# A second-layer quarter moved behind four columns of the next batch's first layer, and a second layer that starts in another PSUM bank

## The chip, the cores and the metric

The kernel runs on one core of a Trainium2 chip. The metric is the device time of one execution in microseconds (us), taken over five runs. Engines are named as in the profile: PE multiplies matrices, PEld loads its weights, DVE is the vector engine, ACT the scalar engine, POOL (GpSimd) issues the loads, SP issues the transposing DMAs and the stores.

## The reference

Eight batches of 448 tokens, 12 heads of 64, so d_model is 768; d_ff is 3072. Squared-ReLU attention, then a layer norm, a two-layer network and a residual:

```python
scores = scale * np.matmul(q, k.transpose(0, 1, 3, 2))
attn = np.maximum(scores, 0.0) ** 2 / S
x = np.matmul(attn, v)                       # then heads side by side: (B, S, 768)
mu, var = np.mean(x, -1), np.mean((x - mu) ** 2, -1)
xn = (x - mu) / np.sqrt(var + 1e-06) * g_ln
out = x + np.maximum(xn @ w_ch1, 0.0) @ w_ch2
```

All products run in bf16 with fp32 sums.

## The kernel before

The program is written out by hand, engine by engine: each engine executes its instructions in the order in which the Python code emits them, and waits on semaphores for what it needs. So a line of Python that is emitted earlier stands earlier in the queue of its engine.

The network of batch b and the attention of batch b+1 run interleaved. `ffn_1_all(b)` (L842) loops over the 24 columns `ni` of the hidden layer, each 128 of the 3072 hidden units. A column is 12 matmuls (L447): six slices `ki` of d_model, times two halves of 64 output partitions that run side by side on the array. ACT then evicts the column with a ReLU into row `ni` of `h` (L449). Between the columns stand "excursions" (L836): three score products of the next batch (L296, L301), their ReLU by ACT (L311, L305) and DVE (L307) and their squares by DVE (L314), and the products with v (L331). In batch 1 they stand behind columns 3, 6, 9, 13, 15, 18 and 21 (`IN_SECOND`).

From batch 2 on the last four columns are computed by `unit` (L649) with seven products instead of eight, in four PSUM banks called c, d, a and e; its products are L660, its evictions L671 to L690. Bank e is read for the last time by DVE at L687, bank c at L676, bank a by the second L671.

The second layer of batches 1 to 7, `ffn_2_all` (L935), takes pairs of 128-token tiles and does each pair in seven products (L515) of 24 matmuls, in three banks that go around. Their order is this line (L941), where x and y are the two banks of the turn `f_turn` and z is `spare[0]`:

```python
banks = [x_bank, z_bank, y_bank]
```

After `unit`, x is its bank c, y its bank e and z its bank a. Batch 4 alone has one pair; there the kernel skips one bank of the turn (`next_f()`, L943), so that the next column starts in the other one.

The second layer of batch 0, `ffn_2_first` (L904), is done plainly, because the weights of the second layer `w2` are still arriving: blocks B11, B21, B12 and B22, 1152 KB each, are loaded by POOL in this order (L214). `plain_part` (L489) does one part of the 24 slices of the hidden layer for tile m and half dh of the output; parts are quarters. For dh=1 the order is m0 and m1 with the first two quarters (block B12), then m0 and m1 with the last two (block B22). Each tile's sum stays in one bank of the turn until DVE evicts it (`scaled_plus`, L482). Between the parts stand the centering of batch 1's input on DVE (L411), a copy of 192 columns of `h` (`carry`, L458) and sums of weight blocks on DVE (`w2_sums`, L218), which batch 1's seven products need.

What feeds the scores of the next batch is a chain of DMAs: POOL loads q and k of a head pair i into one of three slots of `qk_ring` (L175 to L177), SP transposes them into `qkT` (L260, three buffers), PE reads that. The loads of pair i+3 wait until pair i is transposed. On SP's queue also stand the transposes into `x_tok` (L424) and the stores (L475); those of batch 0 are held back until column 9 of batch 1 (`held_stores`, L880).

Of the kernel before, what the change touches and what calls it, by code (L numbers as in the profile page):

```python
# [11 lines left out]
def kernel(  # L12
# [11 lines left out]
    P = 128  # L24
# [3 lines left out]
    Alu = mybir.AluOpType  # L28

    B, H, S, D = q.shape  # L30
# [12 lines left out]
    K2 = d_ff // P  # L43
    KH = K2 // 2
# [37 lines left out]
    w2 = big_pool.tile([P, 7, KH, HD], bf16)  # L82
    B11, B22, B12, B21, B_SUM, B_TOP, B_BOT = range(7)
# [44 lines left out]
    next_f = f_turn.next  # L128
    spare = fb[2:]
# [86 lines left out]
    def w2_sums(slot, a, b, op, part):  # L216
        r = slice(part * KH // 2, (part + 1) * KH // 2)
        nc.vector.tensor_tensor(w2[:, slot, r], w2[:, a, r], w2[:, b, r], op=op)  # L218
# [195 lines left out]
    def tiles_of(b):  # L414
        return range(b * S // P, (b + 1) * S // P)

    def x_slot(m):
        b = next(b for b in range(B) if m in tiles_of(b))
        return m - tiles_of(b)[0] + (0 if b % 2 else 4)
# [6 lines left out]
    def x_carry(b):  # L426

        nc.scalar.copy(xT[:, :, :D], x_first[:, :, S - D:] if b == 0 else xT[:, :, S:])
# [13 lines left out]
    def ffn_1(ni, bank=None):  # L442
        ps = (next_f() if bank is None else bank)[:, :S]
        for ki in range(K1):
            for c in range(2):
                n0 = ni * P + c * D
                nc.tensor.matmul(ps[c * D:(c + 1) * D, :], w1[:, ki, n0:n0 + D], xc[:, ki, :],  # L447
                                 start=(ki == 0), stop=(ki == K1 - 1))
        nc.scalar.activation(h[:, ni, CARRY:], ps, Act.Relu)  # L449

    def h_cols(b, m):
        c0 = CARRY + m * P - b * S
        return slice(c0, c0 + P)
# [6 lines left out]
    def new_o():  # L460
        o_t = o_pool.tile([P, HD], fp32, tag="o")
        return o_t

    def new_acc():
        acc_t = acc_pool.tile([P, HD], fp32, tag="acc")
        return acc_t
# [14 lines left out]
    def scaled_plus(o_t, y, m, plus):  # L481
        nc.vector.scalar_tensor_tensor(o_t, y, rstd[:, m:m + 1], plus, op0=Alu.mult, op1=Alu.add)  # L482

    def x_half(m, dh):
        return x_tok[:, x_slot(m), dh * HD:(dh + 1) * HD]

    held_stores = []

    def plain_part(b, m, dh, part, parts, box):  # L489
        if part == 0:  # L490
            box[m] = next_f()[:, :HD]
        n = K2 // parts
        cols = h_cols(b, m)
        for ki in range(part * n, (part + 1) * n):
            slot = ((B11, B12), (B21, B22))[ki // KH][dh]
            for c in range(2):
                t0 = cols.start + c * D
                nc.tensor.matmul(box[m][c * D:(c + 1) * D, :], h[:, ki, t0:t0 + D],  # L498
                                 w2[:, slot, ki % KH, :], start=(ki == 0), stop=(ki == K2 - 1))
        if part == parts - 1:  # L500
            o_t = new_acc() if dh else new_o()
            scaled_plus(o_t, box[m], m, x_half(m, dh))
            held_stores.append(lambda: store(o_t, m, dh * HD, (dh + 1) * HD))

    s_turn = Turns(range(3))
# [222 lines left out]
    ready = []  # L728
# [113 lines left out]
    def ffn_1_all(b):  # L842
        ms = tiles_of(b)
        for ni in range(NI0 if b == 0 else 0, UNIT if b >= UNIT_FROM else K2):
            if b == 0 and ni == NI0:
                ffn_1_first()
            if b == 0 and ni == NI0 + 2:
                x_carry(0)
            if b == 0 and ni == X_AT[0]:

                nc.sync.dma_start(held, h[:1, ni - 1, CARRY:CARRY + 16])
            if b == 0 and ni in X_AT:
                ffn_x(b, X_AT.index(ni))
            if b == 0 and ni == IN_FIRST[-1] + 1:
                flush_loads()
            if b == 0 and ni in V_AT:
                load_v(V_AT[ni])
            bursts = (IN_FIRST, IN_SECOND, IN_REST)[min(b, 2)]
            ffn_1(ni, spare[1] if b < B - 1 and ni in bursts and len(ready) > 1 else None)
            flush()  # L860
            at = STATS_AT[min(b, 2)][:len(ms)]
            if ni in at:
                ffn_stats(ms[at.index(ni)])
            if b >= UNIT_FROM:
                for n in X_SUMS_AT.get(ni, ()):
                    x_sum(n)
            if b == 1 and ni in SUMS_AT:
                w2_sums(*LATE_SUMS[SUMS_AT.index(ni)])
            if b == 0:
                if ni in IN_FIRST:  # L870
                    excursion(3)
                if ni == IN_FIRST[-1] + 3:
                    next_AV(bank=spare[1])
                if ni in T_IN_FIRST:
                    att_T(NPAIR + T_IN_FIRST[ni])
            elif b < B - 1:
                if ni in bursts:
                    first = nc.vector if b > 1 and ni == bursts[0] else nc.scalar
                    excursion(3, third=(first, nc.vector), **(dict(evac_by=nc.scalar) if b == 1 else {}))
                    while ni > bursts[1] and held_stores:  # L880
                        held_stores.pop(0)()
                if b == 1 and ni == K2 - 1:
                    flush_loads()
                    next_AV(bank=spare[1])

        late = []

        def between(n):
            if n == 2:
                flush_loads()  # L890
            if n == 3:
                next_AV(bank=sc_turn.items[0][:, 0], evac_by=nc.scalar, later=late)
            if n == 5:
                posts.extend(late)

        if b >= UNIT_FROM:
            unit(between)

    CENTER_AT = (4, 6, 8)
    SUMS_AT = (0, 1, 2, 4, 7, 11)  # L900
    LATE_SUMS = [(o, x, y, op, part)
                 for o, x, y, op in ((B_BOT, B21, B22, Alu.add), (B12, B12, B22, Alu.subtract),
                                     (B21, B21, B11, Alu.subtract)) for part in range(2)]
    def ffn_2_first():  # L904
        b = 0
        ffn_rstd(b)
        box = {}
        assert not ready
        steps = center(1)
        n = 0  # L910
        for dh in range(2):

            order = [(m, part) for m in range(2) for part in range(4)]
            if dh:
                order.sort(key=lambda x: x[1] // 2)
            for m, part in order:
                plain_part(b, m, dh, part, 4, box)
                if n < K1 - 1:
                    gain(1, n)
                if n == 3:  # L920
                    gain(1, K1 - 1)
                if n in CENTER_AT:
                    steps[CENTER_AT.index(n)]()
                if n == 2:
                    for ki in range(K1):
                        ffn_x(1, ki)
                if n == 8:
                    carry(b)
                if n in (9, 10):
                    w2_sums(B_TOP, B11, B12, Alu.add, n - 9)  # L930
                if n in (13, 15):
                    w2_sums(B_SUM, B11, B22, Alu.add, (n - 13) // 2)
                n += 1

    def ffn_2_all(b):  # L935
        ffn_rstd(b)
        x_bank, y_bank = f_turn.items
        z_bank = spare[0]
        first = b * S // (2 * P)
        pairs = range(first, (b + 1) * S // (2 * P))  # L940
        banks = [x_bank, z_bank, y_bank]  # L941
        if len(pairs) == 1:
            next_f()  # L943
        todo = []
        if b < B - 1:
            assert not ready
            todo = [lambda k=k: (gain(b + 1, k), gain(b + 1, k + 1)) for k in range(0, K1, 2)]
            todo += center(b + 1)
            if b % 2:
                todo.append(lambda: x_carry(b + 1))  # L950

        def between(n):
            n += 7 * (pr - first)
            if n == (8 if len(pairs) == 2 else 1):
                carry(b)
                if b < B - 1:
                    for ki in range(K1):
                        ffn_x(b + 1, ki)
            if todo:
                todo.pop(0)()  # L960
            if b == UNIT_FROM - 1 and n >= 8 and n < 13:
                w1_sum(n - 8)

        for pr in pairs:
            last = b == B - 1 and pr == pairs[-1]
            seven(b, pr, banks, last, between)
            banks = banks[1:] + banks[:1]
        assert not todo
# [70 lines left out]
```

## Time and profile before

| | |
|---|---|
| median of 5 runs | 521.96 us (521.66 to 522.72) |
| the profiled execution's own time | 522.72 us |
| its span, first to last instruction | 520.6 us, so 2.1 us lie around it |
| PE busy | 510.5 us (98%), granted clock 1.00 throughout |
| DVE busy | 390.3 us (75%) |
| ACT busy | 288.5 us (55%) |
| POOL busy | 224.3 us (43%) |

The times of instructions below come from the one profiled execution and count from its first instruction. A matmul's row shows when it starts and when its result is through; the next one starts well before that, so a PE that reads busy all the time can still lose time between two starts. "Idle before" in a row of the timeline is counted from the end of the last instruction, and is shown from 0.15 us on.

### The profile page before, as it was taken

To read this page: it belongs to the slowest core of one execution; us is meant where nothing else is said; L and a number is where in the kernel's file an instruction comes from. 1 tells how busy PE (TensorE), PEld (TensorE's weight loads), DVE (VectorE), ACT (ScalarE), POOL (GpSimd) and SP (SyncE) were. 2 spreads that over 40 slices of the span, in tenths; PEclk is the share of its full clock that TensorE was granted. 3 is DMA by queue.
4 is the path that set the end of the run, shared out by engine and by line. 5 is a ranking of instruction groups with operands and counts; after the bars stand their busy time and mean duration, and the time that the engine had idled before them with its cause. 6 is when DMAs were issued, how large, how long until landed. Compare 5 with 4: busy or idle time off the path is not lost.

```text
span 520.6 us, 14156 instructions
## 1 busy us (share of the span) xinstructions
PE 510.5 (98%) x5902; PEld 344.2 (66%) x5902; DVE 390.3 (75%) x696; ACT 288.5 (55%) x489; POOL 224.3 (43%) x257
## 2 busy tenths in 40 slices
PE   8999999999999999999999999999999999999996
PEld 4355566546765588755887558655886558877885
DVE  6966779868988689687886868987796867970554
ACT  6986632786248762487524875577525774244220
POOL 9727114778533753248432485257532000320031
PEclk9999999999999999999999999999999999999999
DMA  9999999999537992579924799279924300240022
GB/s 134 181 199 200 184 204 157 147 198 111 82 88 108 121 83 66 117 72 134 82 69 102 77 129 137 64 88 112 85 69 101 62 1 3 79 106 1 3 62 62
DMA packets 175280, 53.05 MB, mean 102 GB/s; under 512 B 154224, under 2 KB 175216, under 8 KB 175216
## 3 DMA queue, kind: packets, MB, share of 16 engines
q0 software_dynamic: 103712, 25.75, 52.9%
q1 hardware_dynamic: 70976, 26.03, 27.0%
q8 instruction: 46, 0.75, 0.6%
q10 hardware_dynamic: 528, 0.37, 0.2%
q14 instruction: 18, 0.15, 0.1%
HBM read 51.91 MB, written 11.01 MB: 121 GB/s over the span
## 4 chain that ended last, share of the span: by engine, by line
PE 80%; DMA 13%; POOL 3%; ACT 2%; DVE 1%; issue 1%; POOLq 0%; ACTq 0%
PE f L515 34%; PE f L447 31%; DMA w<-in_moe_w_ch_dram 7%; PE f L331 4%; DMA s_sb<-in_v_dram 4%; PE f L660 3%; PE sc L301 3%; PE f L301 1%; DMA qkT_t<-qk_ring 1%; DMA v_ring<-in_v_dram 1%; PE sc L296 1%; PE f L498 1%; DVE s_sb L676 1%; PE sc L331 1%; PE f L354 1%; ACT h L675 1%
## 5 line engine op out<-in xcount | busy, mean ns | idle before, releaser
L447 PE MATMUL f<-xc,w 128*64 128x448 bf16 x1968 | 198.3, 353 | 0.3
L447 PEld LDWEIGHTS <-w 128*64 128x64 bf16 x1968 | 114.8, 110 | 76.6 <-issue 15.1
L449 ACT ACTIVATE h<-f 128x448 bf16<-128x448 f32 x164 | 90.3, 551 | 75.3 <-PE f L447 70.2
L515 PE MATMUL f<-w,s_sb 128*64 128x384 bf16 (+2 forms) x1584 | 130.4, 324 | 0.0
L515 PEld LDWEIGHTS <-s_sb 128*64 128x64 bf16 x1584 | 107.9, 110 | 19.3
L311 ACT ACTIVATE at<-sc 128x896 bf16<-128x896 f32 x120 | 103.0, 917 | 5.6 <-PE sc L301 5.1
L314 DVE TENSOR_TENSOR at<-at 128x896 bf16<-128x896 bf16 x168 | 96.8, 619 | 6.9 <-ACT at L311 6.2
L548 POOL TENSOR_TENSOR o_t<-o_t,x_tok 128x384 f32<-128x384 f32 x26 | 24.9, 956 | 153.9 <-ACT o_t L547 153.9
L175 POOL DMA_DIRECT2D qk_ring<-in_q_dram x36 | 46.7, 1298 | 82.0 <-DMA qkT_t<-qk_ring 56.6
L547 ACT ACTIVATE o_t<-f,rstd 128x384 f32<-128x384 f32 x26 | 15.1, 581 | 94.7 <-DVE acc_t L552 37.1
L509 DVE TENSOR_TENSOR s_sb<-h 128x1536 bf16<-128x1536 bf16 x65 | 64.3, 1005 | 0.0
L176 POOL DMA_DIRECT2D qk_ring<-in_k_dram x36 | 55.8, 1550 | 11.1 <-DMA w<-in_moe_w_ch_dram 11.1
L515 PE MATMUL f<-w,h 128*64 128x384 bf16 x624 | 53.2, 326 | 0.9 <-DVE s_sb L676 0.2
L177 POOL DMA_DIRECT2D qk_ring<-in_k_dram x36 | 46.9, 1303 | 4.8 <-DMA w<-in_moe_w_ch_dram 4.7
L515 PEld LDWEIGHTS <-h 128*64 128x64 bf16 x624 | 42.7, 110 | 9.3 <-issue 1.9
L307 DVE TENSOR_SCALAR at<-f 128x448 bf16<-128x448 f32 x59 | 35.6, 616 | 15.0 <-PE f L301 15.0
L548 POOL TENSOR_TENSOR acc_t<-acc_t,x_tok 128x384 f32<-128x384 f32 x24 | 29.0, 1216 | 21.3 <-ACT acc_t L547 21.3
L187 POOL DMA_DIRECT2D v_ring<-in_v_dram x36 | 32.5, 1170 | 0.5 <-DMA qk_ring<-in_q_dram 0.3
L331 PE MATMUL f<-at,v_ring 128*64 128x448 bf16 x248 | 31.1, 357 | 1.2 <-DMA v_ring<-in_v_dram 1.2
L411 DVE SCALAR_TENSOR_TENSOR xc<-f,g_sb,xc 128x448 bf16<-128x448 f32 x45 | 28.5, 678 | 4.6 <-PE f L405 4.6
L301 PE MATMUL sc<-qkT_t 64*128 64x448 bf16 x192 | 30.0, 356 | 0.0
L370 DVE TENSOR_SCALAR xT<-f 128x448 bf16<-128x448 f32 x22 | 13.6, 617 | 18.4 <-ACT at L311 9.8
(111 smaller groups left out, 525.9 us busy)
## 6 DMA issues: line engine op xcount, KB each, us to landing
w<-in_moe_w_ch_dram POOLq DMA_DIRECT2D x6, 768.0 KB, 13.0
w<-in_moe_w_ch_dram POOLq DMA_DIRECT2D x4, 1152.0 KB, 29.5
v_ring<-in_v_dram POOLq DMA_DIRECT2D x21, 192.0 KB, 5.2
qk_ring<-in_q_dram POOLq DMA_DIRECT2D x36, 112.0 KB, 5.1
qk_ring<-in_k_dram POOLq DMA_DIRECT2D x36, 96.0 KB, 4.9
out_dram<-o_t SPq DMA_DIRECT2D x8, 168.0 KB, 2.2
out_dram<-acc_t SPq DMA_DIRECT2D x7, 168.0 KB, 2.2
out_dram<-o_t SPq DMA_DIRECT2D x8, 144.0 KB, 2.1
```

The lines of the kernel that those rows point to most:

```text
L175: nc.gpsimd.dma_start(q_to, q[b, heads].rearrange("x (p j) d -> p j x d", j=NJ))
L176: nc.gpsimd.dma_start(k_to[:, :NF], k[b, heads, :SF].rearrange("x (p t) d -> p t x d", t=NF))
L177: nc.gpsimd.dma_start(k_to[:SS, NF], k[b, 2 * a:2 * a + 2, SF:].rearrange("x s d -> s x d"))
L301: nc.tensor.matmul(by_j(half[hh]), k_of(i, r, t, P), q_of(i, r), start=True, stop=True)
L311: nc.scalar.activation(at, ps[:, :, :S], Act.Relu)
L314: nc.vector.tensor_mul(attn[i, t], attn[i, t], attn[i, t])
L331: nc.tensor.matmul(ps[hh * D:(hh + 1) * D, :], weights, values, start=start, stop=stop)
L447: nc.tensor.matmul(ps[c * D:(c + 1) * D, :], w1[:, ki, n0:n0 + D], xc[:, ki, :], start=(ki == 0), stop=(ki == K1 - 1))
L449: nc.scalar.activation(h[:, ni, CARRY:], ps, Act.Relu)
L509: nc.vector.tensor_tensor(s_sb[:, n], x, y, op=op)
L515: nc.tensor.matmul(ps[c * D:(c + 1) * D, :d1 - d0], stat[:, ki, c * D:(c + 1) * D], w2[:, slot, ki, d0:d1], start=(start and ki == 0), sto ...
L548: nc.gpsimd.tensor_tensor(o_t, o_t, x_half(m, dh), op=Alu.add)
```

## The change

In batch 0's second layer, half dh=1 stops after the two quarters that use block B12; DVE evicts each of the two partial sums with the residual into an fp32 tile (`first_halves`). The two quarters that use B22 become a sum of their own, in banks taken anew from the turn, and run behind column 3 of batch 1's first layer (`ffn_2_first_rest`), ahead of the excursion there; a second `scaled_plus` adds them to the tile. The weight sum B_SUM moves from between those quarters into batch 1's columns 1 and 2, and B_BOT moves from columns 0 and 1 to column 3, where the first half of the new B12 (before at column 2) stands too.

In all later second layers the three banks start with y in place of x. The skipped turn after batch 4 is gone; instead the first column of batch 5 takes `spare[1]`.

```diff
     held_stores = []
+    first_halves = {}
 
     def plain_part(b, m, dh, part, parts, box):
-        if part == 0:
+
+        parted = dh and part == parts // 2
+        if part == 0 or parted:
             box[m] = next_f()[:, :HD]
...
                 nc.tensor.matmul(box[m][c * D:(c + 1) * D, :], h[:, ki, t0:t0 + D],
-                                 w2[:, slot, ki % KH, :], start=(ki == 0), stop=(ki == K2 - 1))
+                                 w2[:, slot, ki % KH, :], start=ki == 0 or bool(dh and ki == KH),
+                                 stop=ki == K2 - 1 or bool(dh and ki == KH - 1))
+        if dh and part == parts // 2 - 1:
+            first_halves[m] = new_acc()
+            scaled_plus(first_halves[m], box[m], m, x_half(m, dh))
         if part == parts - 1:
-            o_t = new_acc() if dh else new_o()
-            scaled_plus(o_t, box[m], m, x_half(m, dh))
+            o_t = first_halves[m] if dh else new_o()
+            scaled_plus(o_t, box[m], m, first_halves[m] if dh else x_half(m, dh))
             held_stores.append(lambda: store(o_t, m, dh * HD, (dh + 1) * HD))
...
-            ffn_1(ni, spare[1] if b < B - 1 and ni in bursts and len(ready) > 1 else None)
+
+            late = ni == 0 and b > 1 and b * S // (2 * P) - (b - 1) * S // (2 * P) == 1
+            ffn_1(ni, spare[1] if late or b < B - 1 and ni in bursts and len(ready) > 1 else None)
...
-            if b == 1 and ni in SUMS_AT:
-                w2_sums(*LATE_SUMS[SUMS_AT.index(ni)])
+            if b == 1:
+                for n, part in enumerate(p for p, at in zip(LATE_SUMS, SUMS_AT) if at == ni):
+                    if ni == REST_AT and n < 2:
+                        ffn_2_first_rest(n)
+                    w2_sums(*part)
...
-    SUMS_AT = (0, 1, 2, 4, 7, 11)
+
+    REST_AT = 3
+    SUMS_AT = (1, 2, 3, 3, 3, 4, 7, 11)
     LATE_SUMS = [(o, x, y, op, part)
-                 for o, x, y, op in ((B_BOT, B21, B22, Alu.add), (B12, B12, B22, Alu.subtract),
-                                     (B21, B21, B11, Alu.subtract)) for part in range(2)]
+                 for o, x, y, op in ((B_SUM, B11, B22, Alu.add), (B_BOT, B21, B22, Alu.add),
+                                     (B12, B12, B22, Alu.subtract), (B21, B21, B11, Alu.subtract))
+                 for part in range(2)]
...
         for dh in range(2):
-
-            order = [(m, part) for m in range(2) for part in range(4)]
-            if dh:
-                order.sort(key=lambda x: x[1] // 2)
-            for m, part in order:
+            for m, part in [(m, part) for m in range(2) for part in range(2 if dh else 4)]:
                 plain_part(b, m, dh, part, 4, box)
...
                 if n in (9, 10):
                     w2_sums(B_TOP, B11, B12, Alu.add, n - 9)
-                if n in (13, 15):
-                    w2_sums(B_SUM, B11, B22, Alu.add, (n - 13) // 2)
                 n += 1
 
+    def ffn_2_first_rest(m):
+        for part in (2, 3):
+            plain_part(0, m, 1, part, 4, box_rest)
+
+    box_rest = {}
...
-        banks = [x_bank, z_bank, y_bank]
-        if len(pairs) == 1:
-            next_f()
+        banks = [y_bank, z_bank, x_bank]
```

## The prediction

> **What bounds the kernel now.** First the page's busy line: which engine fills the span.
>
> ```profile
> PE 510.5 (98%) x5902; PEld 344.2 (66%) x5902; DVE 390.3 (75%) x696; ACT 288.5 (55%) x489; POOL 224.3 (43%) x257
> ```
>
> PE does. The change gives PE the same matmuls, so only PE's waits can change. Next, PE's waits from 40 us on (total, times, longest):
>
> ```profile
> PE f L498 <- DMA w<-in_moe_w_ch_dram: 0.8, 1, 0.8
> PE sc L296 <- DMA qkT_t<-qk_ring: 0.5, 1, 0.5
> PE f L515 <- DVE s_sb L676: 0.2, 1, 0.2
> ```
>
> Three places: block B22 landing late, pair 17's transposed q and k landing late, and a PSUM bank that DVE frees late. This view counts idle time from the end of the last matmul; I count from start to start, with PE's timeline (start, length, instruction). Around B22 and around pair 17:
>
> ```profile
> 72.75 6.99 PE L498 MATMUL f<-w,h 128*64 128x384 bf16 x84
> 80.50 4.09 PE L498 MATMUL f<-w,h 128*64 128x384 bf16 x48 [0.76 <-DMA w<-in_moe_w_ch_dram]
> 84.40 4.73 PE L447 MATMUL f<-xc,w 128*64 128x448 bf16 x48
> 89.06 0.55 PE L301 MATMUL sc<-qkT_t 64*128 64x448 bf16 x4
> ...
> 113.03 0.35 PE L296 MATMUL sc<-qkT_t 64*64 64x448 bf16 x2
> 113.84 0.38 PE L296 MATMUL sc<-qkT_t 64*64 64x448 bf16 x2 [0.46 <-DMA qkT_t<-qk_ring]
> ```
>
> The 48 matmuls of L498 start at 80.50 and the next kind at 84.40, so a pair (two halves side by side) takes 3.90 / 24 = 0.163 us, while one lasts 0.326. The last pair before the wait ended at 79.74, so it started at 79.41 and the next could have started at 79.575: B22 costs 80.50 - 79.575 = 0.93 us. The four L296 at 104.32 all start within 0.01 us, so the wait at 113.04 costs 0.80 us. The chain of waits names its cause, a transpose that SP issued at 107.64 and that landed at 113.80.
>
> The third place is at the end of FFN1's seven products, here in batch 2 (PE, then DVE):
>
> ```profile
> 187.08 0.74 PE L660 MATMUL f<-s_sb,w 128*64 128x224 bf16 x12
> 187.97 2.30 PE L515 MATMUL f<-w,h 128*64 128x384 bf16 x26
> ...
> 185.97 0.62 DVE L687 TENSOR_TENSOR s_sb<-f,s_sb 128x448 f32<-128x448 f32 x1
> 187.29 0.62 DVE L676 TENSOR_TENSOR s_sb<-s_sb,f 128x448 f32<-128x448 f32 x1 [0.70 <-ACT h L675]
> 188.71 0.62 DVE L671 CUSTOM_DVE_ANT_0 h<-f,s_sb 128x448 bf16<-128x448 f32 x1
> ```
>
> Six pairs of L660, 0.259 us each, end at 187.82: the last starts at 187.56, they step by 0.095, the next could start at 187.655. It starts at 187.97, 0.06 after L676 let go of bank c at 187.91: 0.315 us lost. The same pair of rows stands in batches 3 to 6 (0.14 idle before each); in batch 7 (487.37 and 488.34, idle 0.20) it is 0.37. Batch 5's first column has a like wait (PE, then DVE):
>
> ```profile
> 327.77 3.77 PE L515 MATMUL f<-w,s_sb 128*64 128x384 bf16 x44
> 331.68 2.46 PE L447 MATMUL f<-xc,w 128*64 128x448 bf16 x24
> ...
> 329.90 1.27 DVE L411 SCALAR_TENSOR_TENSOR xc<-f,g_sb,xc 128x448 bf16<-128x448 f32 x2
> 331.08 0.55 DVE L571 TENSOR_TENSOR acc_t<-f,acc_t 128x384 f32<-128x384 f32 x1
> ```
>
> The last L515 ended at 331.54, so it started at 331.21 and the next could start at 331.37. It waits for L571, which frees its bank at 331.63: 0.31 us.
>
> **The change part by part**, against the profiled execution's own 522.72 us (span 520.6 and 2.1 around it).
>
> *B22's wait goes:* -0.93 us. By column 3, B22 has long landed (80.46).
>
> *A new wait comes in its place.* Batch 1's columns 0 and 1 take the banks of m0 and m1, now right behind the B12 quarters. Those banks are freed by two new `scaled_plus`, and DVE has this in its queue:
>
> ```profile
> 77.60 1.42 DVE L458 COPY h<-h 128x2304 bf16<-128x2304 bf16 x2
> 78.93 2.62 DVE L218 TENSOR_TENSOR w<-w 128x2304 bf16<-128x2304 bf16 x2
> 82.68 0.62 DVE L482 SCALAR_TENSOR_TENSOR acc_t<-f,rstd,x_tok 128x384 f32<-128x384 f32 x1 [1.12 <-PE f L498]
> 83.21 1.35 DVE L218 TENSOR_TENSOR w<-w 128x2304 bf16<-128x2304 bf16 x1
> ```
>
> The first is emitted before the two B_TOP sums (L218), the second behind them. So: m0's L482 at 78.93, ends 79.55; next instruction 0.53 later (82.68 to 83.21), B_TOP at 79.46 and 80.73 (step 2.62 - 1.35 = 1.27), m1's L482 at 82.00, ends 82.62. With 0.06 from DVE to PE, column 0 can start at 79.61 (0.04 late) and column 1 at 82.68. A column takes 4.66 / 4 = 1.165 us by the rows at 84.40 and 89.06, 1.14 by ACT's evictions, so column 1 would be ready at 80.75: it waits 1.93 us. PE then reaches the excursion behind column 3 by -0.93 + 0.04 + 1.93 = 1.04 us later than before, at 90.1.
>
> *The rest's own cost* on PE is nil: the same 48 matmuls. Its banks are free: columns 2 and 3 are evicted (ACT, 0.54 us) before the rest's first and second tile need them. DVE gains two L482, 1.24 us, and a worse order: behind the rest's first L482 (which waits for PE until 88.3) stand B_BOT, the second L482, B_BOT, B12, in all 88.3 to 93.4; only then the excursion's ReLU (93.9) and squares. Who waits: the third score product behind column 6 needs that ReLU's bank at 94.02 + 1.04 = 95.06, 1.1 us in hand; the products with v at 103.42 + 1.04 = 104.46 need squares that are done by 102.8 (from 93.4 on three excursions' ReLU and squares at 0.53 + 3 x 0.58 us, as at 90.23 and 90.77, and two weight sums of 1.3 between them). If that cover is gone, PE pays the excess one for one. On SP the stores are popped at column 9 as before; the tiles are done by 91, the first store was issued at 101.82. SP and POOL are moved past nothing.
>
> *Pair 17's wait absorbs it.* That chain hangs on no matmul in this stretch: B22 lands at 80.46, q and k load behind it, SP's transposes run from 82.31, the ring's slots come free, and SP's queue brings pair 17's transpose at 107.64. If it lands at 113.80 again, PE's 1.04 us uses up the 0.80: PE goes on at 114.08 in place of 113.84, +0.24 us. How PE stands to this chain in other executions is not seen; the profiled one is the slowest of the five. If the chain is early, up to all 1.04 us stays; if it is later, nothing. I take 0.4, near the row.
>
> *Seven products of batch 1:* no `unit` there, and bank y is column 23's in place of column 22's. ACT evicts column 23 from 122.66 to 123.21; PE starts at 123.21 now. With 0.06 for the handover: +0.06.
>
> *Batches 2 to 7:* bank e is free at 186.59, a microsecond before PE wants it, so five times 0.315 and 0.37 go: -1.95. What is next late: the second product, 24 matmuls or 1.96 us on, needs bank a (z), free at 189.33; it would start at 187.655 + 1.96 = 189.62. 0.29 us in hand, less the handover. The third needs bank c, free since 187.91. If z were late, at most those 0.3 us would be lost again.
>
> *Batch 5's first column* in `spare[1]`, last read by L411 (329.90 to 331.17), which it awaits anyway for its input: -0.31, as 331.37 is still behind 331.23. The removed turn and this column leave the turn as it was.
>
> The sum: 0.4 + 0.06 - 1.95 - 0.31 = -1.80 us, so 520.9 of 522.72. The profiled execution lies 0.76 over the median, and nothing here says which part of it; I take the change off the median: 521.96 - 1.80 = 520.2.
>
> One rule speaks against this change, and the sum doesn't use it. The rows first: POOL issues pair 15's loads at 88.76 and 89.60, 0.84 us apart, while DVE is within four weight sums (85.16 to 90.32); pair 18's at 104.57 and 105.41, again 0.84, while DVE is idle (104.03 to 105.97). The Trainium skill, "SBUF — State Buffer", on the shared port pair and the trap that DVE blocks DMA, says that a DVE instruction in a two-port mode locks GpSimd out, so that it cannot write the descriptors of the DMAs that it issues. By that rule the sums moved to 88.8 to 93.4 would hold back the loads that pair 17's chain hangs on; by the rows they don't.
>
> **Rivals.**
>
> *The loads are held after all (slower).* If POOL's burst of nine loads from 88.76 on had to stand behind DVE's new unbroken stretch, it would start at 93.4, 4.6 us later, and pair 17 would land at 118.4: +4.6 + 0.06 - 1.95 - 0.31 = +2.4, so 524.4. It decides from a delay of 2.2 us on (below that the other gains cover it). Against it stand the two equal spacings. Chance 0.09.
>
> *FFN2's first product finds another wait (no change).* If the bank is not what held it, the 1.95 stays lost: 0.4 + 0.06 - 0.31 = +0.15, so 522.1. For it: L676 is also an ordinary step of DVE's queue. Against it: PE starts 0.06 after L676 in all six batches, and the first product reads rows 0 to 11 of `h`, written long before. Chance 0.13.
>
> *The new wait doesn't arise (faster, as if DVE kept up).* Then PE would come to pair 17 by 0.89 us early, wait there, and go on at 113.84: 0.06 - 1.95 - 0.31 = -2.2, so 519.8. DVE's unbroken queue from 75.88 to 81.55 speaks against it. Chance 0.1.
>
> **How the numbers follow.** My forecast has 0.68: 0.61 with pair 17's chain near where it was, 0.07 with all of the 1.04 us kept (1.04 + 0.06 - 1.95 - 0.31 = -1.16) and a little more lost to DVE's order. About 0.2% (1.0 us) is what a measurement of this kernel tells from no change. Faster by more: 0.61 + 0.1 = 0.71. Within it: 0.13 and 0.07, 0.2. Slower: 0.09. The range: its low end is 519.8 less 0.3 for the spread of a median; its high end takes the full 1.04 us (520.8) and half of the 1.95 lost to bank z (521.7). It leaves out the slower rival and most of the second.
>
> **What would show it.** Right: L498's wait for the DMA is gone from PE's waits; in its place L447 waits for DVE L482 by some 1.6 us of idle time at about 81; L296's wait for qkT is gone or below 0.2; L515's start follows L660's by 0.6 in batches 2 to 7 and no wait for L676 is left; batch 5's first column follows within 0.2. Wrong: POOL's loads behind 88.7 spaced wider than 0.84 us, pair 17's transpose issued later than 108, PE waiting for L307 or L314 between 90 and 105, or L515 waiting for L671.

## The result, and the profile after

The changed kernel takes 519.94 us in the median against 521.64 for the kernel before: ratio 0.9974, 95% interval 0.9967 to 0.9980, so 1.0 to 1.7 us faster. Forecast were 520.2 us and 1.8 us less, taken off the 521.96 of the first five executions.

The profiled execution of the changed kernel was no ordinary one. It took 524.26 us, more than any other of that kernel, with a span of 522.2. The page's first lines, the clock's row of its slices, and a table by stretches (columns: stretch and length, busy time and instructions of PE, PEld, DVE, ACT, POOL, granted clock, share and rate of the DMAs):

```profile
span 522.2 us, 14162 instructions
PE 513.6 (98%) x5902; PEld 319.9 (61%) x5902; DVE 390.4 (75%) x698; ACT 288.7 (55%) x489; POOL 224.3 (43%) x257
PEclk9999998999999999999999999999999999999999
```

```profile
78.00:85.00 7.00, 4.98 (x60) 3.22 (x56) 7.00 (x10) 0.54 (x1) 3.69 (x5) 1.00 1.94 143
85.00:88.50 3.50, 3.50 (x20) 2.24 (x21) 2.45 (x2) 0.54 (x1) 0.59 (x1) 0.51 1.43 205
88.50:92.00 3.50, 3.50 (x42) 2.81 (x40) 0.00 (x0) 1.09 (x2) 3.50 (x6) 1.00 1.66 121
```

PE has the same 5902 matmuls but 3 us more of busy time. Of these, 1.7 us lie between 85.0 and 88.5, where it ran at half clock. (It had also started batch 0's second layer 1.88 us late, at 69.56 in place of 67.68: the trace's record of a full clock begins at 13.4 us, before at 5.2.) The cause of the dip stands in PE's timeline, which answers to the rows at 72.75 to 89.06 of before:

```profile
81.91 1.32 PE L447 MATMUL f<-xc,w 128*64 128x448 bf16 x12 [0.29 <-DVE acc_t L482]
84.97 5.28 PE L447 MATMUL f<-xc,w 128*64 128x448 bf16 x36 [1.74 <-DVE acc_t L482]
90.05 4.09 PE L501 MATMUL f<-w,h 128*64 128x384 bf16 x48
94.08 0.55 PE L301 MATMUL sc<-qkT_t 64*128 64x448 bf16 x4
```

The wait for block B22 is gone. In its place column 1 (84.97) waits for DVE's second eviction, as forecast; the 36 matmuls behind it took 5.08 us (84.97 to 90.05) where they take 3.40 at full clock (83.12 to 86.52 in the next profile).

The same kernel profiled once more, in an execution of 520.92 us (span 518.9) without the dip, PE and then DVE:

```profile
80.06 1.33 PE L447 MATMUL f<-xc,w 128*64 128x448 bf16 x12
83.12 3.60 PE L447 MATMUL f<-xc,w 128*64 128x448 bf16 x36 [1.74 <-DVE acc_t L482]
86.52 4.09 PE L501 MATMUL f<-w,h 128*64 128x384 bf16 x48
90.55 0.55 PE L301 MATMUL sc<-qkT_t 64*128 64x448 bf16 x4
...
78.06 1.42 DVE L458 COPY h<-h 128x2304 bf16<-128x2304 bf16 x2
79.39 0.61 DVE L482 SCALAR_TENSOR_TENSOR acc_t<-f,rstd,x_tok 128x384 f32<-128x384 f32 x1
79.92 2.61 DVE L218 TENSOR_TENSOR w<-w 128x2304 bf16<-128x2304 bf16 x2
82.45 0.61 DVE L482 SCALAR_TENSOR_TENSOR acc_t<-f,rstd,x_tok 128x384 f32<-128x384 f32 x1
```

The copy, eviction, two B_TOP sums, eviction: the second ends at 83.06 and PE goes on at 83.12. Column 0's last pair started at 81.03 and a column's pairs step by 0.19, so 1.90 us are lost.

The later second layers, in this execution's batch 2 and before batch 5 (PE, with DVE's step between; line numbers below L489 have moved by up to 13, L660 is L667, L515 is L522, L676 is L683):

```profile
187.96 0.74 PE L667 MATMUL f<-s_sb,w 128*64 128x224 bf16 x12
188.53 1.79 PE L522 MATMUL f<-w,h 128*64 128x384 bf16 x19
...
188.17 0.62 DVE L683 TENSOR_TENSOR s_sb<-s_sb,f 128x448 f32<-128x448 f32 x1 [0.33 <-ACT h L682]
...
325.73 5.69 PE L522 MATMUL f<-w,s_sb 128*64 128x384 bf16 x68
331.25 0.92 PE L447 MATMUL f<-xc,w 128*64 128x448 bf16 x8
```

From the last product of `unit` to the second layer it is now 0.57 us (0.89 before): PE starts at 188.53, while DVE still reads bank c until 188.79. Batch 5's first column starts 0.16 us after the last L522, with no idle time.

Cutting each trace at PE's first matmul of batch 0's second layer, its first of batch 1's, and its last of all gives two stages that can be compared over kernels (us, each from the timelines):

| | batch 0's FFN2 to batch 1's | from there to the end |
|---|---|---|
| before | 55.53 | 392.43 |
| the change, first profile | 57.75 | 390.06 |
| the change, once more | 55.93 | 390.06 |

The second stage is 2.37 us shorter, to the hundredth in both. The first is longer by 0.40, or by 2.22 with the dip. So in these profiles the banks bring the whole gain, and the moved quarter gives a part of it back; the experiments take the two apart.

### The profile page after: what moved, and what is told of

Its sections match the earlier page's. It is cut to its first block, busy times and chain, and to the rows that moved or that the text cites. A ratio compares the mean times of both kernels' runs of the same rounds, so it can differ in the third digit from the quotient of the medians.

```text
span 522.2 us, 14162 instructions
## 1 busy us (share of the span) xinstructions
PE 513.6 (98%) x5902; PEld 319.9 (61%) x5902; DVE 390.4 (75%) x698; ACT 288.7 (55%) x489; POOL 224.3 (43%) x257
## 4 chain that ended last, share of the span: by engine, by line
PE 82%; ACT 1%; DVE 0%; issue 0%
PE f L522 34%; PE f L447 32%; PE f L667 5%; PE f L331 4%; PE sc L301 3%; PE f L301 1%; PE sc L296 1%; PE f L501 1%; PE sc L331 1%; PE f L354 1%; ACT at L311 0%; PE f L405 0%; ACT h L449 0%; DVE acc_t L482 0%; ACT at L305 0%
## 5 line engine op out<-in xcount | busy, mean ns | idle before, releaser
L447 PE MATMUL f<-xc,w 128*64 128x448 bf16 x1968 | 200.0, 356 | 2.1 <-DVE acc_t L482 2.0
L447 PEld LDWEIGHTS <-w 128*64 128x64 bf16 x1968 | 111.4, 110 | 83.6 <-issue 17.0
L522 PE MATMUL f<-w,s_sb 128*64 128x384 bf16 (+2 forms) x1584 | 130.0, 324 | 0.0
L522 PEld LDWEIGHTS <-s_sb 128*64 128x64 bf16 x1584 | 92.4, 110 | 34.7
L176 POOL DMA_DIRECT2D qk_ring<-in_k_dram x36 | 56.3, 1565 | 12.3 <-DMA w<-in_moe_w_ch_dram 12.3
L522 PE MATMUL f<-w,h 128*64 128x384 bf16 x624 | 52.9, 326 | 0.0
L177 POOL DMA_DIRECT2D qk_ring<-in_k_dram x36 | 47.8, 1327 | 5.3 <-DMA w<-in_moe_w_ch_dram 5.2
L522 PEld LDWEIGHTS <-h 128*64 128x64 bf16 x624 | 36.5, 110 | 13.5
```

The lines of the kernel that those rows point to most:

```text
L176: nc.gpsimd.dma_start(k_to[:, :NF], k[b, heads, :SF].rearrange("x (p t) d -> p t x d", t=NF))
L177: nc.gpsimd.dma_start(k_to[:SS, NF], k[b, 2 * a:2 * a + 2, SF:].rearrange("x s d -> s x d"))
L522: nc.tensor.matmul(ps[c * D:(c + 1) * D, :d1 - d0], stat[:, ki, c * D:(c + 1) * D], w2[:, slot, ki, d0:d1], start=(start and ki == 0), sto ...
```

## The experiments

Theory A is the prediction's: all the gain is in the banks; the moved quarter trades B22's wait for a longer one behind DVE, and the transposes of pairs 12 to 17 take up what PE arrives early. Theory B: the moved quarter brings part of the gain.

**The banks alone.** Edit against the kernel before:

```diff
-        banks = [x_bank, z_bank, y_bank]
-        if len(pairs) == 1:
-            next_f()
+        banks = [y_bank, z_bank, x_bank]
...
-            ffn_1(ni, spare[1] if b < B - 1 and ni in bursts and len(ready) > 1 else None)
+            late = ni == 0 and b > 1 and b * S // (2 * P) - (b - 1) * S // (2 * P) == 1
+            ffn_1(ni, spare[1] if late or b < B - 1 and ni in bursts and len(ready) > 1 else None)
```

> The bank order of the second layer and batch 5's first column alone; batch 0's last quarter stays where it was. Theory A (the gain is all in the banks): 0.32 us in each of batches 2 to 7 and 0.3 at batch 5's first column go, 2.2 us faster than before, so faster than the whole change by what the moved quarter costs (0.2 to 1 us, more where the clock dips); PE's waits keep L498's for block B22 and L296's for pair 17, and no wait for L676 is left. Theory B (the moved quarter brings part of the gain): 0.9 to 1.4 us faster, less than the whole change.

Measured: 519.28 against 521.34 us, ratio 0.9960 (0.9946 to 0.9974), 2.1 us faster. Second stage 390.06, first 54.76; PE waits 0.8 for B22 as before, none for L676. In this execution pair 17 did not hold PE, as the row of its four score products shows (0.38 us together, where the kernel before had 0.80 between two of them):

```profile
113.76 0.38 PE L296 MATMUL sc<-qkT_t 64*64 64x448 bf16 x4
```

This run's edits touch nothing ahead of this row, so pair 17's wait, which theory A expected to stay, is not in every execution of the kernel before.

**The quarter alone.** The changed kernel with the old bank order and the skipped turn put back (the diff above reversed).

> The moved quarter alone, banks as before. Theory A: column 1 of batch 1 waits 1.9 us for DVE's second eviction behind the two B_TOP sums; against B22's wait of 0.9 and pair 17's of 0.8 that are saved, 0.2 to 1.0 us slower than before, and 1.7 us more in those executions in which PE's clock halves for 3.4 us at the wait. The profile shows L447 waiting for L482 by some 1.7 us and no wait for B22. Theory B: 0.5 to 0.9 us faster than before.

Measured: 521.79 us, ratio 1.0012 (0.9999 to 1.0025): 0.45 us slower in the median, not resolved from nothing, and no gain. Stages 55.64 and 392.43. PE's waits in its profile, largest first:

```profile
PE f L447 <- DVE acc_t L482: 1.7, 1, 1.7
PE f L708 <- DVE w L109: 1.2, 1, 1.2
```

No wait for B22 or pair 17 is left; L447's took their place. The two halves add up: -2.06 + 0.45 = -1.6 against the -1.7 of the whole. Theory B falls.

**Evictions first.**

```diff
-                if n in (9, 10):
-                    w2_sums(B_TOP, B11, B12, Alu.add, n - 9)
+                if n == 11:
+                    for part_n in range(2):
+                        w2_sums(B_TOP, B11, B12, Alu.add, part_n)
```

> The whole change, with both B_TOP sums emitted behind the second eviction in place of ahead of it. Theory A: L447's wait for L482 goes and with it any dip of the clock; PE comes to pairs 15 and 17 about 0.9 us earlier than before the change and waits there instead (L296 for the transpose, 1.5 us or more in all), so the time is that of the banks alone, 2.2 us faster than before, within 0.3. Rival: the transposes come earlier too, and the 0.9 us is kept, 3.1 us faster than before.

Measured: 519.03 us, ratio 0.9962 (0.9950 to 0.9975), 2.3 us faster in the median: as the banks alone. PE's timeline shows where the saved time stops:

```profile
79.87 4.73 PE L447 MATMUL f<-xc,w 128*64 128x448 bf16 x48
84.41 4.09 PE L501 MATMUL f<-w,h 128*64 128x384 bf16 x48
89.80 0.55 PE L301 MATMUL sc<-qkT_t 64*128 64x448 bf16 x4 [1.30 <-DMA qkT_t<-qk_ring]
```

All four columns run through without a wait, the rest too, and then PE waits 1.3 us for pair 12's transpose, and later 0.5 for pair 17's, counted from start to start (first stage 55.59). Theory A had the absorbing waits at pairs 15 and 17; they stand at 12 and 17, but they absorb.

**Evictions first and the stores late.** In addition:

```diff
-                    while ni > bursts[1] and held_stores:
+                    while ni > bursts[3] and held_stores:
```

> As the one with the evictions first, and batch 0's stores leave SP's queue behind column 15 in place of column 9, so that pair 17's transpose no longer stands behind them. Theory A: pair 17 is transposed at about 104 in place of 107.6 and lands by 110; what is left is pair 15's wait of some 0.5 us, so 1.0 to 1.4 us are gained on top of the banks' 2.2: 3.2 to 3.6 us faster than before. Rival: the chain of loads, not the stores, sets pair 17, and it gains nothing on top, 2.2 us faster.

Measured: 518.30 us, ratio 0.9944 (0.9927 to 0.9962), 3.0 us faster. Pair 17 was transposed at 104.56 and landed at 109.73; no wait for a transpose stands in this profile, and the first stage is 53.71, 1.8 us below that of before. Not all of this is the stores' doing. Beside evictions first the stage is 1.88 us shorter; some 0.5 of it is pair 17's wait, but 1.4 is pair 12's, which in that profile had ended at 89.80, before any store was issued (102.91). The medians of the two, 0.7 us apart, have overlapping intervals, and theory A's 3.2 to 3.6 is not quite reached. Run again (below), it gave 517.98 us, ratio 0.9929 (0.9908 to 0.9950).

**The stores late in the kernel before.** The same edit, nothing else.

> The kernel before with batch 0's stores behind column 15 in place of column 9, nothing else. Theory A (pair 17's transpose stands behind the stores): L296's wait for pair 17 goes, up to 0.8 us faster than before, 0.4 on the average of executions, since some executions don't have it. Rival: the chain of loads sets it, no change.

Measured: 521.18 against 520.99 us, ratio 1.0006 (0.9997 to 1.0015): no gain, so theory A's 0.4 did not come. In its profile pair 17 is early too (landed at 110.09), but PE had waited longer for B22, which this edit does not touch:

```profile
80.81 4.09 PE L498 MATMUL f<-w,h 128*64 128x384 bf16 x48 [1.48 <-DMA w<-in_moe_w_ch_dram]
```

First stage 55.44. A PE that waits 1.6 us for B22 (1.48 idle) comes to pair 17 late anyway. That the two waits are ends of one chain, so that taking away the later one alone brings nothing, fits the median, but is argued from one profile here and not shown.

**The banks and the late stores**, without the moved quarter.

> The banks alone and the late stores, the quarter not moved. Theory A: the two add up, 2.1 to 2.3 and 0.4 to 0.8, so 2.5 to 3.1 us faster than before. Against the kernel with the evictions first and late stores (3.0 faster) it tells what the moved quarter is worth where nothing else holds PE: theory A says that B22's 0.9 then comes through, less 0.5 for pairs 12 and 15, so this one should be 0.3 to 0.6 us slower than that. Rival: the quarter is worth nothing, the same time.

Measured: 519.18 us, ratio 0.9963 (0.9949 to 0.9976), 1.8 us faster; B22's wait 1.48 idle again, stages 55.55 and 390.06. Late stores add nothing here either; theory A's 2.5 to 3.1 us was missed. With the quarter moved and the evictions first the gain is 3.0 us, and 4.0 when run again: by the medians the moved quarter is worth 1 us or more, but only with both other edits. The two were measured on different chips, each beside the kernel before, and the intervals of 3.0 and 1.8 overlap, so the size is not settled.

**A longer wait.** The whole change with B_SUM's two sums ahead of the second eviction as well:

```diff
-    SUMS_AT = (1, 2, 3, 3, 3, 4, 7, 11)
+    SUMS_AT = (3, 3, 3, 4, 7, 11)
...
-                 for o, x, y, op in ((B_SUM, B11, B22, Alu.add), (B_BOT, B21, B22, Alu.add),
+                 for o, x, y, op in ((B_BOT, B21, B22, Alu.add),
...
                     w2_sums(B_TOP, B11, B12, Alu.add, n - 9)
+                    w2_sums(B_SUM, B11, B22, Alu.add, n - 9)
```

> The whole change with its new wait made longer: the two B_SUM sums stand ahead of the second eviction too, 2 x 1.3 us of DVE more. Theory A: column 1 waits 4.5 us in place of 1.9; PE comes to pair 17 late in any case, so nothing is absorbed and all 2.6 us show: 2.6 us slower than the whole change. If a wait of that length also halves PE's clock for 3.4 us in most executions, 1.7 us more: 4.3 slower than the whole change, 2.5 us slower than before. Rival (the wait has cover in the chain of transposes): less than 1 us slower than the whole change.

Measured: 524.03 us, ratio 1.0056 (1.0043 to 1.0068) against before, some 4.5 us slower than the whole change: more than the 2.8 us by which the wait grew (2.6 for the two sums, 0.2 in which the first of them waited for B22, landed at 81.47). PE's timeline, and the stretch in which the clock was low:

```profile
85.97 6.13 PE L447 MATMUL f<-xc,w 128*64 128x448 bf16 x36 [4.55 <-DVE acc_t L482]
```

```profile
84.30:91.10 6.80, 5.12 (x28) 3.12 (x29) 1.62 (x2) 0.94 (x2) 3.01 (x6) 0.50 1.39 142
```

The clock was halved for 6.8 us in the profiled execution (526.04 us). In all six executions the mean granted clock was 0.993 to 0.997; of the whole change's 45 executions whose clock is known, four have 0.997 or less. So the longer wait most likely pays the clock every time; where it was low is seen in the profiled execution alone.

**Pairs 12 to 14 loaded ahead of B22.** On top of evictions first and late stores, the three `load_qk` and the memset of the ring stand ahead of `load_w2(B22, 1, 1)`.

> Evictions first, late stores, and the loads of pairs 12 to 14 queued ahead of block B22's, which nothing needs before 84 us now. Theory A: pairs 12, 15 and 17 land some microseconds before PE wants them, no wait for a transpose is left, and all of B22's 0.93 and pair 17's 0.80 is kept beside the banks' 2.3: 4.0 us faster than before. Rival: block B22, now later by the time of these loads (672 KB, 2 to 3 us), holds up the B_SUM sums on DVE and with them the rest's evictions and the squares, and it is no faster than with the late stores alone (3.0).

Measured: 525.91 us, ratio 1.0092 (1.0078 to 1.0106): 4.9 us slower than before.

```profile
90.56 5.80 PE L501 MATMUL f<-w,h 128*64 128x384 bf16 x48 [6.25 <-DMA w<-in_moe_w_ch_dram]
```

B22 landed at 90.5 in place of 80.5. Not its place on the wires did that but its issue: POOL, which before issued it at 43.74, now did so at 77.03, behind nine small loads; by the semaphores that it waits for, each of them had to wait for the load eight before it, and pair 12's landed only at 76.3. The clock was halved for 6.8 us here too (0.50 from 87.2 on). The rival was right that it is no faster, but by a larger price and another path than it had: not only DVE's sums but PE's own matmuls of the rest waited for B22.

**Pair 12 alone ahead of B22**, and beside it the kernel with the late stores once more.

> Evictions first, late stores, and only pair 12's three loads queued ahead of block B22's. With eight DMA semaphores in turn, B22's load then waits at most for a load of the first layer's weights, and joins the queue at about 50 us in place of 43.7, ahead of its turn on the wires (74.6); it lands some 1.5 us later, at about 82, before PE wants it at 84.4, and pair 12 lands at about 80 in place of 88. Theory A: the executions in which pair 12 or 15 still held PE lose that wait: 0.2 to 0.5 us faster than the same kernel with B22 first, 3.3 to 3.5 us faster than before. Rival: B22 again comes later than that and holds up DVE's sums and PE, slower than with B22 first.

> The kernel with the evictions first and late stores once more, beside the one with pair 12's loads ahead of B22's, so that the two are compared on one chip. 3.0 us faster than before.

Measured: 518.89 against 517.98 us (before: 522.01; ratios 0.9938, 0.9920 to 0.9957, and 0.9929, 0.9908 to 0.9950). B22 landed at 82.20 as expected, pair 12 at 84.26; but pairs 13 and 14, now behind B22, held SP's queue, pair 15's transpose was issued at 98.06, and PE waited for it:

```profile
103.99 0.38 PE L296 MATMUL sc<-qkT_t 64*64 64x448 bf16 x2 [1.48 <-DMA qkT_t<-qk_ring]
```

The 0.2 to 0.5 us that theory A gave it did not come; which of the two is faster is not resolved. The best version measured is evictions first, late stores, B22 first: 3 to 4 us under the kernel before.

**The change once more.** The execution shown above.

> The whole change unaltered, for one more profile: the first one fell on an execution in which PE's clock rose 8 us late at the start and halved at the new wait. Theory A: in an execution without these, from batch 0's second layer to batch 1's it takes 0.1 to 1.0 us more than before, and from batch 1's second layer to the end 2.3 to 2.4 us less; L447 waits for L482 by 1.7 us, nothing waits for L676. The span then is 518 to 519 us. Rival: the clock halves at this wait in every execution, and the first stretch takes 2 us more than before.

Measured: first stage 0.40 us longer than before, second 2.37 shorter, span 518.9. The rival falls: the dip is not in every execution. (This is a single execution, of 520.92 us; the one of the kernel before beside it took 520.68. The gain of the change rests on the medians, not on this pair.)

## Why the prediction was right

*Banks of batches 2 to 7 and batch 5's first column:* forecast -1.95 and -0.31, together -2.26. The stage that holds them all shrank by 2.37 in every profiled kernel that has the new order and by nothing in the others. At the seven waits themselves the step from the last product to the next matmul fell by 0.31 (five times), 0.36 in batch 7 and 0.31 at batch 5's column, as forecast; the other 0.15 us lie in small steps of the matmuls around them. Bank a was never waited for. Shown by the banks alone. The +0.06 at batch 1's second layer falls in the first stage, and came out as 0.05.

*The wait that takes B22's place:* forecast 1.93 us from DVE's rows of the trace before; measured 1.90. Shown by evictions first, in which it is gone. B22's own wait, 0.93 in the trace that I had, was 0.92 in the profile of the banks alone and 1.64 in both profiles with late stores and the quarter in its old place.

*Pair 17's chain takes up the difference:* forecast a net of 0.24 to 1.04 us, 0.4 taken. In the clean profile PE reaches the excursion behind column 3, counted from the stage's start, 1.03 us later than before (forecast 1.04), and ends the stage 0.40 later: pair 17 now costs it 0.27 us in place of 0.80.

```profile
114.39 0.65 PE L296 MATMUL sc<-qkT_t 64*64 64x448 bf16 x4
```

The medians of the quarter alone say 0.45. In this profile the mechanism is as forecast, and evictions first shows time that PE had saved lost again to these transposes. That the size fits to a hundredth is luck: with the quarter in its old place the first stage took 54.76 to 55.55 us in four profiles, and against the shortest of them (the banks alone, without pair 17's wait) the same 55.93 would have read as 1.17 us. So is part of the closeness of 520.2 to 519.94: over 84 executions the kernel before has 521.64, and 1.8 us off that is 519.84.

One of the signs of being wrong did appear, a transpose of pair 17 issued later than 108. In the clean profile it was issued at 108.63, but there B22 had landed at 81.39 in place of 80.46, and the transpose follows it by 27.2 us in both: the chain as a whole came later and was no slower. In the profile with the dip it was issued at 109.89, 30.6 us behind B22, and there one sentence of the prediction was too strong: that this chain hangs on no matmul. Pair 15's transpose was issued at 98.80, 0.4 us after PE's score product of 98.39, for whose buffer it waits; PE was so late that the chain followed PE.

*What was missed is the clock.* No term had it. In the profiled execution it cost 1.7 us (36 matmuls in 5.08 for 3.40). Of 45 executions of the changed kernel whose clock is known, four had a mean of 0.997 or lower; they took 521.24 to 524.26 us, against the median of 519.94. A low mean need not come from this wait: the banks alone had its halving at 11.1 us, and of 51 executions of the kernel before, run beside the experiments, three had a mean of 0.997. How often this wait halves the clock is therefore not known; four in 45 is the most, so the median hardly has it.

*The rivals:* POOL's loads were not held. In the first profile of the change (POOL's timeline), with DVE in L218 from 92.83 to 94.18 and from 94.78 to 97.40:

```profile
91.81 1.82 POOL L177 DMA_DIRECT2D qk_ring<-in_k_dram  x1
92.41 2.38 POOL L175 DMA_DIRECT2D qk_ring<-in_q_dram  x1
93.23 2.66 POOL L176 DMA_DIRECT2D qk_ring<-in_k_dram  x1
94.06 2.44 POOL L177 DMA_DIRECT2D qk_ring<-in_k_dram  x1
```

The starts stay 0.82 and 0.83 us apart. The Trainium skill's rule that DVE blocks such DMAs ("SBUF — State Buffer") speaks of instructions in a two-port mode, and the same page, under "Who interferes with whom", says that `tensor_tensor`, which these sums are, has no such mode. So the prediction was wrong to say that by this rule the sums would hold back the loads; this trace, which shows no delay, agrees with the page. The rival with another wait before FFN2 fell with the 0.57 us step, and the one in which DVE keeps up was made by hand: evictions first, at 2.3 us.

## What to carry to other kernels

Cost a moved piece of work by the queue of the engine that must free its buffers, in the order in which that queue is written: one eviction emitted behind two sums of 1.3 us cost more than the wait that the move was there to remove. Where one chain of transfers seems to feed two waits, expect little from removing either alone (here evictions first and the late stores each added nothing clear, together 1 us or more); remove them together, or look first for waits that recur and hang on nothing, like a bank that another bank of the same turn can stand in for, which paid six times over. And count lost time from start to start: the waits of 0.14 us idle were worth 0.31 each.

## What the hardware showed

A wait of PE that read 1.74 us idle, with 0.29 idle shortly before, was followed by 3.4 us at half clock (0.51 from 85.0 to 88.5) in one profile, and by none in two others with a wait of 1.74 and 1.73 us (the change once more and the quarter alone, each without the 0.29) and none behind the three waits of 1.48 us. In a wait of 4.55 us and one of 6.25 us the halving began some 2.9 us after PE had fallen idle (at 84.3 and 87.2), while it still waited, and lasted 6.8 us. The Trainium skill, "TensorE: Matmul & The Clock Gate", in its part on HAM oscillation, gives as rule that PE should not be idle for more than about 3.4 us; here the length of a dip, 3.4 us or twice that, fits such a window, but one dip came after far less idle time than the rule allows, and in the two long waits the halving came a little earlier than it says.
